# Block-sparse attention with a two-layer network behind it, on one core: the sampled numbers come in one piece, group 0's registers are loaded by two engines, weights are issued behind the first keys, and TensorE is given constant products in the opening

## The chip, the cores and the metric

The kernel runs on 1 core of one Trainium2 chip. The metric is the device time of one execution in microseconds (us), the median of several runs. The engines are named as in the profile: PE (TensorE, matmuls; PEld is its weight load), DVE (VectorE), ACT (ScalarE), POOL (GpSimd) and SP (SyncE, which here only loads registers and issues transfers). SPq, POOLq and PEq are the sequencers of these engines.

## The reference

Four batches, eight heads, 768 positions in 24 blocks of 32. A query block sees its neighbours, the first and the last block, and three sampled blocks; the first and the last query block see everything. The output goes through a two-layer network whose gate is h for h >= 1, 0 for h <= -1 and (h+1)^2/4 between.

```python
scores = scale * np.matmul(q, k.transpose(0, 1, 3, 2))
mask = np.abs(blk_i - blk_j) <= window
mask = mask | (blk_i == 0) | (blk_j == 0) | (blk_i == n_blocks - 1) | (blk_j == n_blocks - 1)
for qb in range(n_blocks):
    for kb in sampled_blocks[qb]:
        mask[qb * block:(qb + 1) * block, kb * block:(kb + 1) * block] = True
scores = np.where(mask, scores, -1000000000.0)
attn = np.exp(scores - np.max(scores, axis=-1, keepdims=True))
attn = attn / (np.sum(attn, axis=-1, keepdims=True) + 1e-09)
x = np.matmul(attn, v)           # then (4, 8, 768, 64) -> (3072, 512)
h = x @ w_in                     # (512, 2048), given in float64
g = np.where(pos, h, np.where(neg, 0.0, (h + beta) ** 2 / (4.0 * beta)))
out = g @ w_out                  # (2048, 512), given in float64
```

## The kernel before, in words

The work is cut into 24 **groups** of 128 queries (six for each batch), and the groups into nine **chunks** of two or three. Chunk 0 is the groups 0, 1 and 2. For a chunk the network runs 16 times over 128 of its 2048 hidden columns: `l1` (L628 to L630, 12 products into a bank `h` or `ob`), the gate (ACT L633, L635, L638; DVE L636; DVE or POOL L640) and `l2` (L647 to L649, into `oa`). The attention of the next chunk is interleaved with the network of this one. Chunk 0's attention has nothing to stand beside it but the conversion of the weights: it is the **opening**, and it ends with the first `l1` (67.61 us in the profile).

A group loads its queries `q` and, for the first group of a batch, the keys `kn` (two halves of 768 KB). The sampled block numbers are brought into `sreg` by a transfer (L182), and SP and POOL load 12 of them for a group into registers (L303). With these SP gathers value blocks into `va` or `vx` (L355, 64 KB each, 12 for a group), and POOL copies the sampled key blocks into `kr` (L345, 12 copies of 128x128 for a group, 6 into `kr0` and 6 into `kr1`). `ends` (L330) puts the first and the last key block into `kr`. Then two **score rounds** of matmuls go into two banks (`sa` and `sb`, or `oa1` and `oa2` for group 1), each followed by two minima (DVE L411), four exponentials (ACT L414), four transposes (PE L419) and copies of the turned tiles `pt` (L422). `values` multiplies with the values (L166, into `ob` or `oa0`), `xn` (DVE L570) divides, PE turns it back (L578), and `x` is written in a high (ACT L583) and a low part (DVE L584). `l1` of a chunk needs `x` of all its groups.

The weights come as float64. A **conversion** takes a tile of 1 MB (into one of three raw buffers: `stg0`, `stg1` and `out4`) through ACT L237, DVE L238, L240, L242 and L244, and splits it into a high part (ACT L247) and a low part (L249 on DVE or POOL). There are 16 of them, 8 for `w_in` and 8 for `w_out`; `w_out` also goes to DRAM as `wo_dram` for the later chunks.

The order of all steps on all engines is written out: `ORDER` is a packed list of step numbers that `Plan.order` unpacks, and the body runs the steps in it, so each engine's queue is that list in order. `BY` picks the engine of those steps that have a choice. The durations written at `pe(...)`, `act(...)` and so on are a planner's costs; nothing at run time reads them.

Of the kernel before, what the change touches and what calls it, by code (L numbers as in the profile page):

```python
# [24 lines left out]
NP = H // 2  # L25
# [48 lines left out]
def body(ctx, tc, q_t, k_t, v, samp, moe_w_in, moe_w_out, cst_in, out):  # L74
# [51 lines left out]
    sreg = sb.tile([1, NB * NR], I32, name="sreg")  # L126
# [46 lines left out]
    def constants():  # L173
# [84 lines left out]
    def group(b, t, key, wide, lead):  # L258
# [26 lines left out]
        if t == 0:  # L285
            for s in range(2):
                bs = slice(12 * s, 12 * s + 12)
                load(at(0) - lead + KNL[s], KN[:, bs], k_t[b, :, bs], ["first"] if g else (), [("kn", 3 * s + k) for k in range(3)], size=786432, by=None if g else ACT)
# [13 lines left out]
        def values_of(name, engine):  # L302
            vals[name] = nc.values_load_multi_w_load_instructions(  # L303
                sreg[0:1, blocks[0] * NR:(blocks[-1 if not mixed else 1] + 1) * NR], engines=[engine], min_val=0, max_val=NB - 1,
                skip_runtime_bounds_check_because="the sampled numbers are numbers of key blocks")[1]

        add("SP", 2.6, at(0) - lead + 3.4, lambda: values_of("SP", mybir.EngineType.SP), ["sreg"], [("val", "SP", g % 2)], 0.1)
        pool(1.6, at(0) - 1.6, lambda: values_of("POOL", mybir.EngineType.Pool), ["sreg"], [("val", "POOL", g % 2)], port=False, lat=1.1)
        for hf in range(nh):
# [32 lines left out]
            def keys(n=n, hf=hf):  # L342
                for m, val in enumerate(vals["POOL"][2 * NR * hf:2 * NR * hf + 2 * NR]):
# [3 lines left out]
            pool(1.72, at(0) - 1.5 + hf, keys, [("val", "POOL", g % 2)] + [("kn", s) for s in range(6)], [krn])  # L347
# [80 lines left out]
        if not mixed:  # L428
            for rnd in range(2):
                items = [(e, 2 * rnd + a, 256 * a, c, slice(32 * c, 32 * c + 32), i, c)  # L430
                         for a in range(2) for c, i in enumerate(blocks) for e in range(2)]
                pe((2.0, 1.5)[chunk] if narrow else 1.11, at(0.28 * rnd), lambda items=items: score_parts(items), score_reads, list(sn))
# [27 lines left out]
            pe(3.2 if chunk == 0 else 2.5 if chunk == 1 else 1.95, at(0.66), values, [("pt", p) for p in range(NP)] + va_r + vb_r, [on] + ([("vxdone", g - 1)] if spread else []))  # L460
# [134 lines left out]
    def moe(c, fis, t0, p, between):  # L595
# [5 lines left out]
        for k, fi in enumerate(fis):  # L601
            u = t0 + k * p
            for at_k, part in between:
                if at_k == fi:
                    attention(1, part)
# [106 lines left out]
    with tc.manual_schedule():  # L712
        for i in seq:
            plan.steps[i][3]()
# [6 lines left out]
BY = ("11200011100110000001011102100111000000000000001000000000000000000000001101100010011000110001101010101111010110"  # L721
      "11111111001110101010000000010111100000000000000000000000000000000000000000000000000000000000000000000000000000"
# [3 lines left out]
LEAD_0, LEAD_C, LEAD_W, LEAD_A, AHEAD = -33.59, 22.83, 5.97, 2.71, 7.29  # L726
L2 = 2.31
# [3 lines left out]
c-jrugMwf=5CFh*(#l)gwr$U>ZQHhO+qP}nwr$(qyZVb_V~sInoDq}PfSGOLnJ`9;H(^a7gC?5EXJVUhCYFh7qL?{msflhPn7O8e$!+4Bc_zGRXJVR!CNMEf  # L731
0+ZOBHc?GdGv6dKNlY@cz@#$EOe7P>EH;tNa#P+!G)qhhv(V%*-Ax6P+N3mTOmdUfEHdd#dz0Q|G!@NylfjfVl}sj+*%UFAO*WIo6gE{&U8rV?niVFisbWf-
l_t~_H>=DBli$=dZA^Ak+mthF%|=tq)H3T#8ME4KG9f01S!0sfI;NzlYjT=WX0vHv8k#01m-%V7nChmVX=`ej`li3BXPTO=rn%W}wwZ#akr`n6n8s#@8E86~
# [102 lines left out]
```

## Time and profile before

| | before |
|---|---|
| runs shown | 792.92, 794.43, 796.32 us; median 794.43 us |
| the profiled execution | 791.04 us, of which the span from the first to the last instruction is 789.3 us |
| PE busy | 753.5 us, 95% of the span |
| DVE, ACT, POOL busy | 363.5, 408.6, 138.6 us |
| mean granted clock of PE | 0.983 of full speed |

Idle time of PE and stretches at half clock are what a span can lose; the stages with most of both are read from windows of the trace. The page's shares of the whole span say little of the opening, which is less than a tenth of it.

### The profile page before, as it was taken

Reading aid. Unit: us, or ns where it says so; the run is one execution under the profiler, and the core shown is the slowest. Engines: PE = TensorE matmul, PEld = TensorE weight load, DVE = VectorE, ACT = ScalarE, POOL = GpSimd, SP = SyncE. Lnnn points to the kernel's source line nnn. Section 1 sums busy time; section 2 is a strip of 40 time slices with the busy share of each in tenths; the row PEclk is TensorE's granted clock in tenths of the full one; section 3 lists DMA queues with packets and bytes.
Section 4 is the critical chain, followed back from the end, with each engine's and each line's share of the span. In section 5 each row is a group of like instructions: output and inputs, shape, how many; then the busy total and the mean of one; then the engine's idle time right before and its main releaser. Section 6 shows DMA issues by size and latency. Waiting matters only on the chain.

```text
span 789.3 us, 21997 instructions
## 1 busy us (share of the span) xinstructions
PE 753.5 (95%) x8880; PEld 643.3 (82%) x8880; DVE 363.5 (46%) x695; ACT 408.6 (52%) x994; POOL 138.6 (18%) x379
## 2 busy tenths in 40 slices
PE   4788989999999999999999999999999999999997
PEld 3567868888878888888888888888888888888995
DVE  3956989633543334343443444344434242444332
ACT  1776677556755444444554454544545444546442
POOL 3242100304434100032220210032202020100000
PEclk7889999999999999999999999999999999999999
DMA  8998979587687365665466465755554636553554
GB/s 270 240 272 255 314 258 318 183 247 266 203 226 234 134 188 172 188 213 189 161 187 195 131 198 161 198 193 183 188 164 163 185 121 188 166 166 125 173 187 147
DMA packets 60457, 156.89 MB, mean 199 GB/s; under 512 B 8900, under 2 KB 9156, under 8 KB 60356
## 3 DMA queue, kind: packets, MB, share of 16 engines
q1 hardware_dynamic: 59924, 153.66, 61.9%
q10 hardware_dynamic: 432, 1.84, 0.7%
q8 instruction: 70, 1.15, 0.6%
q14 instruction: 31, 0.25, 0.1%
HBM read 140.78 MB, written 14.68 MB: 197 GB/s over the span
## 4 chain that ended last, share of the span: by engine, by line
PE 84%; DVE 5%; DMA 4%; ACT 3%; issue 3%; POOLq 1%; POOL 0%; SPq 0%; ACTq 0%
PE oa L647 11%; PE oa L649 10%; PE oa L648 10%; PE h L628 9%; PE h L630 9%; PE h L629 9%; PE sa L166 7%; PE ob L166 6%; PE ptb L419 5%; PE sb L166 1%; PE oa L628 1%; PE oa L630 1%; PE oa L629 1%; PE ptb L578 1%; DMA stg<-in_moe_w_out_dram 1%
## 5 line engine op out<-in xcount | busy, mean ns | idle before, releaser
L647 PE MATMUL oa<-w,gh 128*128 128x512 f32 x384 | 160.2, 417 | 1.7 <-DMA w<-wo_dram 1.3
L649 PE MATMUL oa<-w,gl 128*128 128x512 f32 x384 | 151.7, 395 | 0.1
L648 PE MATMUL oa<-w,gh 128*128 128x512 f32 x384 | 151.0, 393 | 0.0
L628 PE MATMUL h<-x,wi 128*128 128x384 f32 (+1 forms) x432 | 145.9, 338 | 2.2 <-DVE r L636 1.3
L633 ACT ACTIVATE r<-h,half_c 128x384 f32<-128x384 f32 (+1 forms) x108 | 60.8, 563 | 167.1 <-PE h L630 166.3
L630 PE MATMUL h<-x,wi 128*128 128x384 f32 (+1 forms) x432 | 141.4, 327 | 0.1
L629 PE MATMUL h<-x,wi 128*128 128x384 f32 (+1 forms) x432 | 140.7, 326 | 0.0
L636 DVE SCALAR_TENSOR_TENSOR r<-r,h 128x384 f32<-128x384 f32 (+1 forms) x108 | 56.8, 526 | 110.1 <-ACT r L635 109.2
L638 ACT CAST gh<-r 128x384 fp32r<-128x384 f32 (+1 forms) x144 | 68.5, 476 | 68.2 <-DVE r L636 60.9
L628 PEld LDWEIGHTS h<-x,wi 128*128 128x128 f32 x432 | 81.3, 188 | 10.2 <-issue 2.2
L647 PEld LDWEIGHTS oa<-w,gh 128*128 128x128 f32 x384 | 72.6, 189 | 20.8 <-issue 6.0
L337 POOL COPY kr<-kn 128x384 f32<-128x384 f32 x56 | 28.9, 547 | 341.1 <-PE sb L166 232.9
L649 PEld LDWEIGHTS oa<-w,gl 128*128 128x128 f32 x384 | 72.4, 189 | 17.1 <-DVE gl L640 0.6
L640 DVE TENSOR_TENSOR gl<-r,gh 128x384 fp32r<-128x384 f32 (+1 forms) x123 | 65.6, 534 | 42.4 <-ACT gh L638 38.6
L629 PEld LDWEIGHTS h<-x,wi 128*128 128x128 f32 x432 | 81.4, 188 | 2.0 <-DVE x L584 0.2
L648 PEld LDWEIGHTS oa<-w,gh 128*128 128x128 f32 x384 | 72.8, 190 | 10.8
L630 PEld LDWEIGHTS h<-x,wi 128*128 128x128 f32 x432 | 81.2, 188 | 0.4 <-issue 0.4
L345 POOL COPY kr<-kn 128x128 f32 x264 | 70.1, 315 | 43.2 <-PE sb L166 31.9
L635 ACT ACTIVATE r<-r 128x384 f32<-128x384 f32 (+1 forms) x144 | 70.8, 492 | 3.0
L166 PE MATMUL sa<-kr,q 64*32 64x256 f32 (+1 forms) x672 | 52.8, 382 | 9.7 <-POOL kr L345 8.3
L166 PE MATMUL sb<-kr,q 64*32 64x256 f32 (+1 forms) x672 | 52.3, 382 | 2.9 <-issue 2.6
L419 PE MATMUL ptb<-cst,p 128*128 128x128 f32 x328 | 51.2, 277 | 3.9 <-ACT pt L422 2.3
(143 smaller groups left out, 1244.2 us busy)
## 6 DMA issues: line engine op xcount, KB each, us to landing
w<-wo_dram SPq DMA_DIRECT2D x128, 512.0 KB, 3.4
va<-in_v_dram SPq DMA_DIRECT2D x240, 64.0 KB, 4.0
vb<-in_v_dram SPq DMA_DIRECT2D x38, 384.0 KB, 4.7
wo_dram<-w SPq DMA_DIRECT2D x16, 512.0 KB, 7.8
stg<-in_moe_w_in_dram SPq DMA_DIRECT2D x6, 1024.0 KB, 7.3
stg<-in_v_dram SPq DMA_DIRECT2D x8, 768.0 KB, 6.3
q<-in_q_t_dram SPq DMA_DIRECT2D x23, 256.0 KB, 4.4
stg<-in_moe_w_out_dram SPq DMA_DIRECT2D x5, 1024.0 KB, 8.5
```

Source lines behind the costliest of these rows:

```text
L166: PE.matmul(out=o, lhsT=l, rhs=r, start=start, stop=True, skip_group_check=True)
L345: POOL.tensor_copy(out=KR[n][:, m // NR, s:s + 1], in_=KN[:, bass.ds(val, 1)])
L419: PE.transpose(out=bank[:, k * 128:k * 128 + 128], in_=s, identity=ident)
L628: PE.matmul(out=h, lhsT=win(j, 0, fs), rhs=x[:, j, 0, 0:nt], start=(j == 0), stop=False)
L629: PE.matmul(out=h, lhsT=win(j, 0, fs), rhs=x[:, j, 1, 0:nt], start=False, stop=False)
L630: PE.matmul(out=h, lhsT=win(j, 1, fs), rhs=x[:, j, 0, 0:nt], start=False, stop=(j == NP - 1))
L635: act(GATE[size[c]][1], u, lambda r=r: ACT.activation(out=r, in_=r, func=AF.Square), [("r", n2)], [("r", n2)])
L638: act(GATE[size[c]][3], u, lambda r=r, gh=gh: ACT.copy(out=gh, in_=r), [("r", n2)], [("gh", n3)])
L640: return lambda: eng.tensor_tensor(out=gl, in0=r, in1=f(gh), op=ALU.subtract)
L647: PE.matmul(out=oa[t], lhsT=gh[:, ts], rhs=w[:, 0], start=(fi == fis[0]), stop=False)
L648: PE.matmul(out=oa[t], lhsT=gh[:, ts], rhs=w[:, 1], start=False, stop=False)
L649: PE.matmul(out=oa[t], lhsT=gl[:, ts], rhs=w[:, 0], start=False, stop=(fi == fis[-1]))
```

## The change

- `sreg` becomes twice as long and takes the sampled numbers as they lie in DRAM, 576 bytes in one piece, where before 72 words of 4 bytes were picked out of it. The registers are then loaded from every second word.
- Group 0's numbers for `kr1` are loaded into registers of ACT, and ACT makes the six copies into `kr1`. POOL loads six numbers for group 0 in place of twelve.
- `first`, on which the loads of weights and values wait in the planner's list, is now written by SP's register load for group 0 and not by the first transfer. So the weights are issued behind it; the keys and the queries of group 0 don't wait for it.
- `FILL` inserts 27 products of a constant tile (128x128 by 128x384, float32) ahead of six steps of PE: 7 before the first score round, then 5, 8, 2, 3 and 2. Nothing reads what they write.
- The costs of score rounds and of `values` in the opening are lower, and `ORDER` and `BY` are new tables: all queues have another order.

```diff
-    sreg = sb.tile([1, NB * NR], I32, name="sreg")
+    sreg = sb.tile([1, 2 * NB * NR], I32, name="sreg")
...
         def numbers():
-            SP.dma_start(out=sreg, in_=low(s_lin)[:, :, 0])
+            SP.dma_start(out=sreg, in_=s_lin.bitcast(I32))
             SP.dma_start(out=sraw, in_=s_lin.bitcast(I32).to_broadcast([128, 2 * NB * NR]))
 
-        add("SP", 2.2, -70, numbers, (), ["sreg", "sraw", "first"], size=80000)
-        load(-64, cst, cst_in, ["first"], ["cst"], size=200000)
+        add("SP", 1.2, -70, numbers, (), ["sreg", "sraw", "issued"], size=80000)
+        load(-64, cst, cst_in, ["issued"], ["cst"], size=200000)
...
+        nv = 2 * NR * nh
+        add("SP", 2.6, at(0) - lead + 3.4, lambda: values_of("SP", mybir.EngineType.SP, 0, nv), ["sreg"], [("val", "SP", g % 2)] + (["first"] if g == 0 else []), 0.1)
+        if g:
+            pool(2.4, at(0) - 1.6, lambda: values_of("POOL", mybir.EngineType.Pool, 0, nv), ["sreg"], [("val", "POOL", g % 2)], port=False, lat=0.4)
+        else:
+            pool(1.6, at(0) - 1.6, lambda: values_of("POOL", mybir.EngineType.Pool, 0, 2 * NR), ["sreg"], [("val", "POOL", 0)], port=False, lat=0.1)
+            act(1.6, at(0) - 1.6, lambda: values_of("ACT", mybir.EngineType.Activation, 2 * NR, nv), ["sreg"], [("val", "ACT", 0)])
...
+            by_act = g == 0 and hf == 1
+
+            def keys(n=n, hf=hf, who="ACT" if by_act else "POOL", copy=ACT.copy if by_act else POOL.tensor_copy):
+                for m in range(2 * NR):
                     s = m % NR + (5 if g == 1 else 0)
-                    POOL.tensor_copy(out=KR[n][:, m // NR, s:s + 1], in_=KN[:, bass.ds(val, 1)])
+                    copy(out=KR[n][:, m // NR, s:s + 1], in_=KN[:, bass.ds(vals[who][2 * NR * hf + m], 1)])
...
         for i in seq:
+            for _ in range(FILL.get(i, (0, 0))[0]):
+                PE.matmul(out=oa[FILL[i][1]][:, 0:HALF], lhsT=f(GH[0])[:, 0:128], rhs=f(GH[0]), start=True, stop=True)
             plan.steps[i][3]()
...
+FILL = {31: (7, 1), 38: (5, 1), 51: (8, 1), 82: (2, 1), 100: (3, 0), 136: (2, 1)}
```

PE's queue, from its first instruction to the transposes of group 0's second score round; `L724` is the constant product, `oa_112` is `oa1`, and the line numbers of the changed kernel are 7 to 12 higher.

```order
 L199 MATMUL h<-gh_71 128x384 x16
+L724 MATMUL oa_112<-gh_71 128x384 x7
 L166 MATMUL sa<-kr_80,q_77 32x160
...
-L419 MATMUL h<-cst,p_86 128x128 x2
-L419 MATMUL h<-cst,p_87 128x128 x2
+L724 MATMUL oa_112<-gh_71 128x384 x5
+L428 MATMUL h<-cst,p_86 128x128 x2
+L428 MATMUL h<-cst,p_87 128x128 x2
...
+L724 MATMUL oa_112<-gh_71 128x384 x8
```

Seven products were put between the warm-up and the first scores, five between these and the first transposes, eight ahead of the second round's transposes.

ACT's queue in the changed kernel behind its first transfers, up to group 0's four exponentials (L423; the `p` are the four tiles of the first round).

```order
L304 TENSOR_LOAD sreg
L337 COPY kr_81<-kn 128x256 x2
...
L354 COPY kr_81<-kn 128x128
...
L337 COPY kr_80<-kn 128x256 x2
L237 ACTIVATE stg_96<-stg_96 128x2x512
L423 ACTIVATE p_86,sm_97<-sa,nm_100 128x256
L423 ACTIVATE p_88,sm_97<-sa,nm_100 128x256
L237 ACTIVATE stg_95<-stg_95 128x2x512
L423 ACTIVATE p_87,sm_97<-sb,nm_100 128x256
L423 ACTIVATE p_89,sm_97<-sb,nm_100 128x256
```

Before, the same place read as follows.

```order
L330 COPY kr_80<-kn 128x256 x2
L330 COPY kr_81<-kn 128x256 x2
L237 ACTIVATE stg_95<-stg_95 128x2x512
L414 ACTIVATE p_87,sm_97<-sb,nm_100 128x256
L414 ACTIVATE p_89,sm_97<-sb,nm_100 128x256
L414 ACTIVATE p_86,sm_97<-sa,nm_100 128x256
L414 ACTIVATE p_88,sm_97<-sa,nm_100 128x256
L237 ACTIVATE stg_96<-stg_96 128x2x512
```

The register load and the copies into `kr1` are new on ACT (the copy's row stands six times there, an address row ahead of each), and the second weight tile's L237 moved from behind the four exponentials to between them.

SP's queue where group 2's queries (`q_77`) are loaded, in the changed kernel and then before; `vx_84` are group 1's values.

```order
L163 DMA out_76<-in_moe_w_out_dram 128x2x1024
...
L364 DMA vx_84<-in_v_dram 32x512
...
L364 DMA va<-in_v_dram 32x512
L163 DMA q_77<-in_q_t_dram 128x512
L163 DMA stg_95<-in_moe_w_out_dram 128x2x1024
```

```order
L163 DMA out_76<-in_moe_w_out_dram 128x2x1024
...
L355 DMA vx_84<-in_v_dram 32x512
L163 DMA vx_84<-in_v_dram 96x4x512
L163 DMA vx_84<-in_v_dram 32x4x512
L163 DMA q_77<-in_q_t_dram 128x512
```

The load of `q_77` moved ahead of group 1's neighbour values (`96x4x512`, 768 KB), of its two loads of end blocks (256 KB each; the other stood further up) and of one gather.

PE's queue at the end of the opening, with group 2's transposes back (`xn_94`); before, and then changed.

```order
L166 MATMUL sb<-mask,ones 32x2x96
L578 MATMUL h<-cst,xn_94 128x128 x4
L419 MATMUL ptb<-cst,p_88 128x128 x2
L419 MATMUL ptb<-cst,p_89 128x128 x2
L628 MATMUL h<-x_67,wi 128x384
```

```order
L166 MATMUL ob<-vx_85,pt_93 32x64 x16
L587 MATMUL h<-cst,xn_94 128x128 x4
L166 MATMUL sa<-kr_80,q_78 32x160
L166 MATMUL sa<-kn,q_78 32x96
L166 MATMUL sb<-kr_80,q_78 32x160
```

Before, group 3's second score round stood between group 2's `values` and its transposes back; now the transposes come first and the score round stands between them and the first `l1`.

## Rows read from the trace of the kernel before

**Rows 1.** Page: heading, and the granted clock in 40 slices.

```profile
span 789.3 us, 21997 instructions
...
PEclk7889999999999999999999999999999999999999
```

**Rows 2.** Windows by stage: start:end, busy us of each engine, clock, DMA share, GB/s.

```profile
0.00:13.70 13.70, 4.63 (x17) 4.31 (x17) 3.63 (x16) 2.61 (x5) 2.46 (x14) 0.80 0.81 262
13.70:67.60 53.90, 39.63 (x1032) 30.93 (x1032) 35.40 (x54) 32.33 (x88) 21.18 (x55) 0.83 0.90 248
67.60:143.70 76.10, 71.36 (x768) 61.19 (x768) 71.28 (x105) 54.09 (x111) 4.68 (x9) 0.98 0.84 277
...
160.00:770.00 610.00, 608.21 (x6849) 522.46 (x6848) 239.54 (x494) 305.05 (x762) 104.18 (x297) 1.00 0.58 183
770.00:789.30 19.30, 13.41 (x74) 10.87 (x72) 4.46 (x10) 4.90 (x11) 0.00 (x0) 1.00 0.43 141
```

**Rows 3.** Chain that ended last, 0 to 30 us: start us, us, what.

```profile
0.75 4.67 DMA sreg<-in_samp_dram
5.44 2.92 POOLq L303
8.43 2.74 POOLq L303
...
14.83 1.91 POOL kr L345 x4
...
18.87 0.70 DVE nm L411
...
21.12 0.66 PE h L419 x4
```

**Rows 4.** Timeline of ACT in the opening.

```profile
9.93 1.28 ACT L330 ACT_TABLE_LOAD   x1 [9.93 <-DMA kn<-in_k_t_dram]
11.22 1.32 ACT L330 COPY kr<-kn 128x256 f32<-128x256 f32 x4
...
21.41 1.17 ACT L237 ACTIVATE stg<-stg 128x1024 f32<-128x1024 f32 x1
```

**Rows 5.** DMA issues, 0 to 30 us: KB each, median us from issue to landing.

```profile
q<-in_q_t_dram ACTq DMA_DIRECT2D x1, 256.0 KB, 4.5
```

**Rows 6.** Chain that ended last, 30 to 68 us.

```profile
30.34 1.51 issue
...
32.56 6.88 DMA q<-in_q_t_dram
...
40.23 0.44 PE sa L166
...
42.99 1.06 PE h L419 x4
...
60.12 2.65 issue
...
65.16 1.06 PE h L578 x4
...
67.61 0.44 PE h L628
```

**Rows 7.** Windows: the longest stretch at half clock, and four such together.

```profile
9.20:19.40 10.20, 4.54 (x74) 3.35 (x74) 4.54 (x13) 3.76 (x6) 6.72 (x24) 0.55 1.00 303
...
sum 23.80, PE 17.31 PEld 14.23 DVE 10.76 ACT 11.86 POOL 14.38; mean PE 4.33 PEld 3.56 DVE 2.69 ACT 2.97 POOL 3.60
```

**Rows 8.** Timeline of PE: the warm-up.

```profile
1.33 4.63 PE L199 MATMUL h<-gh 128*128 128x384 f32 x16 [1.33 <-DVE ones L193]
```

**Rows 9.** Groups of DVE by shape, 67.6 to 143.7 us: busy us, mean ns.

```profile
L249 DVE TENSOR_TENSOR wi<-stg,wi 128x512 fp32r<-128x512 f32 x12 | 7.9, 683 | 0.0
...
L640 DVE TENSOR_TENSOR gl<-r,gh 128x384 fp32r<-128x384 f32 x11 | 6.0, 551 | 0.0
```

**Rows 10.** Waits of DVE, 13 to 143 us: total us, times, longest.

```profile
DVE stg L238 <- ACT stg L237: 6.6, 4, 2.9
```

More of the change, by code (lines that the diff above doesn't have):

```diff
@@ L287, in group @@
                 bs = slice(12 * s, 12 * s + 12)
-                load(at(0) - lead + KNL[s], KN[:, bs], k_t[b, :, bs], ["first"] if g else (), [("kn", 3 * s + k) for k in range(3)], size=786432, by=None if g else ACT)
+                load(at(0) - lead + KNL[s], KN[:, bs], k_t[b, :, bs], (), [("kn", 3 * s + k) for k in range(3)], size=786432, by=None if g else ACT)
         nh = len(blocks) // 2
@@ L300, in group, with values_of @@
         vals = {}
-        def values_of(name, engine):
-            vals[name] = nc.values_load_multi_w_load_instructions(
-                sreg[0:1, blocks[0] * NR:(blocks[-1 if not mixed else 1] + 1) * NR], engines=[engine], min_val=0, max_val=NB - 1,
+        def values_of(name, engine, lo, hi):
+            numbers = sreg.rearrange("a (n w) -> a n w", w=2)[:, blocks[0] * NR + lo:blocks[0] * NR + hi, 0]
+            got = nc.values_load_multi_w_load_instructions(
+                numbers, engines=[engine], min_val=0, max_val=NB - 1,
                 skip_runtime_bounds_check_because="the sampled numbers are numbers of key blocks")[1]
-        add("SP", 2.6, at(0) - lead + 3.4, lambda: values_of("SP", mybir.EngineType.SP), ["sreg"], [("val", "SP", g % 2)], 0.1)
-        pool(1.6, at(0) - 1.6, lambda: values_of("POOL", mybir.EngineType.Pool), ["sreg"], [("val", "POOL", g % 2)], port=False, lat=1.1)
+            vals.setdefault(name, {}).update(zip(range(lo, hi), got))
+        nv = 2 * NR * nh
[5 more added lines that the diff above has]
+            act(1.6, at(0) - 1.6, lambda: values_of("ACT", mybir.EngineType.Activation, 2 * NR, nv), ["sreg"], [("val", "ACT", 0)])
         for hf in range(nh):
@@ L431, in group @@
                          for a in range(2) for c, i in enumerate(blocks) for e in range(2)]
-                pe((2.0, 1.5)[chunk] if narrow else 1.11, at(0.28 * rnd), lambda items=items: score_parts(items), score_reads, list(sn))
+                pe(1.5 if narrow else 1.11, at(0.28 * rnd), lambda items=items: score_parts(items), score_reads, list(sn))
                 for e in range(2):
@@ L458, in values @@
                             first = False
-            pe(3.2 if chunk == 0 else 2.5 if chunk == 1 else 1.95, at(0.66), values, [("pt", p) for p in range(NP)] + va_r + vb_r, [on] + ([("vxdone", g - 1)] if spread else []))
+            pe(2.3 if chunk < 2 else 1.95, at(0.66), values, [("pt", p) for p in range(NP)] + va_r + vb_r, [on] + ([("vxdone", g - 1)] if spread else []))
             def recip():
@@ L602, in moe @@
             u = t0 + k * p
-            for at_k, part in between:
+            for at_k, one in between:
                 if at_k == fi:
-                    attention(1, part)
+                    attention(1, one)
             if c == 0 and opens and fi % 4 == 0:
```

102 lines of the change are left out of this document (50 added, 52 removed).

## The prediction

> **What bounds the kernel now.** I read the windows by stage first [rows 2]. From 160 to 770 us PE is busy for 608.21 of 610.00 us at full clock: that stage is as long as its matmuls, and the change alters none of them. The last 19.3 us keep their order. From 67.6 to 143.7 us, the network of chunk 0, PE is busy for 71.36 and DVE for 71.28 of 76.10 us: two engines are nearly full, and DMA has a share of 0.84. Only the stage before it is loose. From 13.7 to 67.6 us PE is busy for 39.63 of 53.90 us, so 14.3 us are idle, and the granted clock is 0.83 of full, so part of the busy time runs at half. What the change is worth is thus how much earlier the first `l1` starts, which is at 67.61 us [rows 6], less what the next stage gives back.
>
> Then I followed the chain. It begins with the sampled numbers: 4.67 us for `sreg`, two register loads on POOL of 2.92 and 2.74 us, the key copies until 14.83 + 1.91 = 16.74 us, the minima at 18.87 us and the first transposes at 21.12 us [rows 3]. Later it waits 6.88 us for group 2's queries, stops twice with no releaser shown (1.51 and 2.65 us), and ends with group 2's way back from 65.16 to 67.61 us [rows 6].
>
> The page's clock line has 7 and 8 in its first slices and 9 everywhere after [rows 1]. In the four stretches at half clock that I cut out, PE is busy for 17.31 of 23.80 us [rows 7]; at full clock the same work would take half, so 8.7 us is the most that a warm clock can give.
>
> **The change part by part.**
>
> *First scores.* The numbers in one piece: the price of one short transfer is not in the rows. It lies between nothing saved (4.67 us, if the queue ahead of it sets it) and a landing before the 4.5 us of the queries [rows 5]; I take 4.0 us, landing at 4.75. Six register values at half of the 2.92 us row are 1.5 us, the next twelve 2.74, so POOL is ready at about 9.0 in place of 11.17 us. But the copies also need the second half of the keys, which let ACT go at 9.93 us [rows 4]. With 72 words of four bytes and the weights no longer beside them, I take 9.7 us (8.7 to 9.9). POOL then makes 12 copies before group 0 is complete, group 1's six first by the order. At the pitch before, 24 copies from 11.2 to 16.74 us or 0.23 each, they take 2.8 us. ACT has four end copies of 1.32 us [rows 4] and six key copies. A register-addressed copy on ACT is not in the trace; between 0.23 (POOL's pitch) and 0.33 us (a quarter of 1.32) I take 0.3, so 3.1 us. The inputs are complete at 12.8 us. A score round at half clock took from 40.23 to 42.99 us, 2.76 us [rows 6], so it ends at 15.6 in place of 18.87 us: **3.3 us** earlier. Seven constant products lie in the 7.7 us between the warm-up's end (1.33 + 4.63) and the first score at 13.7. One costs between 0.29 us (the warm-up's 4.63/16, another format [rows 8]) and 0.83 us (three columns' worth of 1.11/4, from the transposes' 1.06 us for four at half clock [rows 6]); I take 0.4, so 2.8 us, and even 5.8 us fits.
>
> *First transposes.* Now the second weight tile's L237, 1.17 us [rows 4], stands between the exponentials. That gives back 1.2 us: **2.1 us** are left. The five products ahead of the transposes take 2 us in a wait that was 21.12 - 18.87 = 2.25 us. Were they at 0.83 us each, they would hold PE for 4.2 us and cost the whole of this gain.
>
> *Group 2's queries.* By the order rows their load is ahead of 768 + 256 + 256 + 64 KB that stood before it. At the 248 GB/s of this stage [rows 2] 1.38 MB are 5.5 us, and PE waited for just these queries. But in the new order group 1's second score round comes after group 2's first one, so one round (2.76 us at half clock) is still to be done there. 5.5 - 2.8 = **2.7 us**; the 2.1 us of the start are in it, not beside it, since both shorten the same path. Ends: 0.7 (if transfers, not order, set the pace) and 5.5.
>
> *Group 2's way back.* Before, the score round of group 3 came first, then the transposes back, and the first `l1` waited 67.61 - 65.16 = 2.45 us for ACT's and DVE's parts of `x`. Now the score round lies between, and covers that: **2.4 us** (0 to 2.4). The 2.65 us stop falls in the same score round; I leave it where it is.
>
> *Clock and constant products.* Twenty products from the first scores on are 8 us at 0.4, laid into 14.3 us of idle time. If they keep the clock up, at most 8.7 us come back. But much of what ran at half clock was followed by a wait for ACT, DVE or a transfer, which the clock doesn't shorten. I take a quarter: **2.2 us** (0 to 8.7).
>
> *DVE behind it.* Counted in the two orders up to the last `l2` of chunk 0, DVE has 27 splits L249 in place of 26, 14 low parts L640 in place of 12, and seven copies of `pt` in place of six. At 0.68 and 0.55 us [rows 9] that is 0.68 + 1.10 + 0.68 = **2.5 us** more, in a stage where DVE is busy for 94%. POOL's and ACT's relief there is worth nothing, since neither is full.
>
> *Sum.* -2.7 - 2.4 - 2.2 + 2.5 = -4.8 us. The profiled execution took 791.04 us with a span of 789.3, so it would be 786.2; it lies 3.4 us below the median of the runs shown, 794.43, which becomes 789.6. I say **789.5 us**. With every term at its good end it would be 14 us less, with every one at its bad end 2 us more; they won't all fall together.
>
> [...]
>
> **The rivals.**
>
> *The gain ends in the weights (0 to 2.5 us less).* DVE and DMA set the next stage: DVE has only 4.8 us of idle time in 76.1, and the raw tiles come when buffers are free. For it: both are near full [rows 2]. Against it: a start that is earlier for all engines shifts the whole stage, and what DVE has to do behind the first `l1` grew by little. Time: about 793.
>
> *All of the clock comes back.* Then the term is 8.7 in place of 2.2 us, the sum -11.3, the time 783. For it: the idle gaps that the products fill are the ones ahead of half clock. Against it: the chain of this stage passes through ACT, DVE and transfers as often as through PE.
>
> *Slower: weight tiles block ACT's queue.* L237 waits for its tile, and ACT works in order. In the new order it stands between group 0's exponentials and again ahead of group 1's; near the end DVE's L238 stands ahead of group 2's low part of `x`. Before, DVE waited for L237 four times, 2.9 us at the longest [rows 10]. If the three places each cost 2.9 us, that is 8.7 us, of which the sum holds 1.2; less the 4.8 us of the forecast, the kernel is 2.7 us slower, with the extra waits of PE at half clock some 4, so about 798. It decides from the point at which group 0's second tile lands later than about 19 us: from there on the first transposes are no earlier than before. Against it: that tile is asked for right behind SP's register load, the first tile and two gathers, some 10 us ahead of that point.
>
> *The numbers' form does nothing*, since the keys land at 9.9 us anyway: that takes 0.2 us off the first term and is inside the range.
>
> **How the numbers follow.** The forecast has 0.52, with a range of its own from 786 to 792; about seven tenths of it lie more than 4 us below 794.4. The gain that ends in the weights has 0.25, all of the clock 0.10, slower 0.13. A measurement of this kernel tells about 0.5%, or 4 us, from no change. Faster: 0.37 + 0.10 = 0.47. Same: 0.15 + 0.25 = 0.40. Slower: 0.13. The range 784 to 796 leaves out most of the full clock's case and most of the slower one, about 2 in 10.
>
> **What would show it.** Right: the first minima at about 15.6 us, the first transposes near 19, group 2's queries landing near 34, the first `l1` at 61 to 63 us, and a DVE that is at least as full behind it. The clock of the 13.7 to 67.6 us stage above 0.83 with a PE that is no less idle would be the products' work. Wrong: exponentials on ACT waiting behind an L237 that waits for its tile; the first `l1` earlier by 5 us and the end of chunk 0 not; or products at half clock that are still running when their transposes could start.

## The result and the profile after

The changed kernel takes **798.97 us** (median of 20 runs, 794.34 to 802.22), the kernel before 794.11 us beside it (20 runs, 788.58 to 799.75). The ratio is **1.0068, 95% interval 1.0048 to 1.0087**: slower by 0.7%, above the range of the prediction.

From the page of the changed kernel: the span, busy times, the granted clock in 40 slices, and the queue that brings TensorE's instructions (packets, MB, share).

```profile
span 795.9 us, 22112 instructions
...
PE 765.4 (96%) x8934; PEld 650.8 (82%) x8934; DVE 372.5 (47%) x705; ACT 408.5 (51%) x995; POOL 132.6 (17%) x368
...
PEclk9998999999999999999999999999999999999999
...
q8 instruction: 70, 1.15, 0.6%
```

The windows that answer to [rows 2], with the same columns:

```profile
0.00:13.70 13.70, 9.65 (x30) 7.45 (x30) 2.54 (x12) 4.20 (x12) 2.44 (x13) 1.00 0.80 259
13.70:67.60 53.90, 41.62 (x952) 31.12 (x952) 35.55 (x57) 28.93 (x79) 14.57 (x38) 0.93 0.83 230
67.60:143.70 76.10, 69.47 (x851) 59.29 (x852) 67.48 (x99) 52.24 (x108) 9.01 (x20) 0.96 0.84 269
160.00:770.00 610.00, 609.19 (x6905) 521.97 (x6904) 246.25 (x506) 304.38 (x761) 103.35 (x297) 1.00 0.60 186
```

The clock did what it was to do: 0.93 in the stage from 13.7 to 67.6 us, 0.83 before. All the same that stage is longer. The first `l1` starts at 74.2 us in place of 67.61, and from there to the end both kernels take the same 721.7 us (795.9 - 74.2, 789.3 - 67.6). So the 6.6 us that the two spans differ by are lost ahead of the first `l1`. The chain of the changed kernel up to there (start us, us, what), which answers to [rows 3] and [rows 6]:

```profile
0.75 1.25 DMA sreg<-in_samp_dram
2.01 2.65 SPq L304
...
7.10 12.52 DMA stg<-in_moe_w_in_dram
19.65 1.12 ACT stg L237
...
23.84 5.16 PE oa L724 x16
...
33.47 1.31 PE ob L166 x50
34.79 2.40 issue
37.19 2.35 PE ob L166 x78
...
41.07 2.29 issue
...
63.14 1.47 PE ob L166 x92
64.61 3.36 issue
67.97 1.30 PE ob L166 x36
```

The numbers land in 1.25 us in place of 4.67, but the chain no longer runs through them. It runs through the second weight tile, which lets ACT's `L237` go at 19.65 us between group 0's exponentials; through eight constant products (`L724`), 5.16 us or **0.645 us each**; and through three stops named issue, 8.05 us together, where before there were two of 1.51 and 2.65 us. Each stop lies inside a step whose operands are there: group 0's values stop after 50 of their 128 matmuls, group 2's after 92. (The chain has a fourth, of 0.82 us at 32.66 us, ahead of the first of group 0's values. It ends at 33.47 us, as group 0's last two gathers land, at 33.38 and 33.57 us.)

The half clock that the changed kernel has ahead of its first `l1` begins at the end of each of these three stops, or within its last 0.7 us, after TensorE has stood still. In these windows the clock is the third number from the end:

```profile
36.60:40.00 3.40, 2.81 (x94) 2.64 (x101) 1.79 (x3) 0.70 (x4) 0.00 (x0) 0.50 1.05 222
43.40:46.80 3.40, 3.40 (x46) 2.72 (x54) 1.19 (x2) 1.11 (x3) 0.00 (x0) 0.51 0.23 78
67.30:74.20 6.90, 5.44 (x116) 4.50 (x117) 4.37 (x6) 1.12 (x2) 1.05 (x3) 0.51 0.83 286
```

ACT's opening, as [rows 4]:

```profile
11.42 0.71 ACT L337 COPY kr<-kn 128x256 f32<-128x256 f32 x2 [7.37 <-DMA kn<-in_k_t_dram]
12.04 1.29 ACT L354 COPY kr<-kn 128x128 f32 x6
...
19.65 1.12 ACT L237 ACTIVATE stg<-stg 128x1024 f32<-128x1024 f32 x1 [1.09 <-DMA stg<-in_moe_w_in_dram]
20.67 0.46 ACT L423 ACTIVATE p<-sb,nm 128x256 f32<-128x256 f32 x1
```

The keys let ACT go at 11.42 us, later than the 9.93 of before. And the group of the products by its shape:

```profile
L724 PE MATMUL oa<-gh 128*128 128x384 f32 x54 | 18.5, 488 | 0.0
```

27 products are 54 matmuls: a product of float32 runs as two matmuls here, each with a weight load of its own (54 too). They are 18.5 us of TensorE, yet its busy time rose by only 11.9 us over the 753.5 of the kernel before, so 6.6 us of other work came back. TensorE's idle time (span less busy) fell from 35.8 to 30.5 us.

### The profile page after: what moved, and what is told of

Read it like the earlier page. It is cut to its first block, busy times and chain, and to the rows that moved or that the text cites. A ratio compares the mean times of both kernels' runs of the same rounds, so it can differ in the third digit from the quotient of the medians.

```text
span 795.9 us, 22112 instructions
## 1 busy us (share of the span) xinstructions
PE 765.4 (96%) x8934; PEld 650.8 (82%) x8934; DVE 372.5 (47%) x705; ACT 408.5 (51%) x995; POOL 132.6 (17%) x368
## 3 DMA queue, kind: packets, MB, share of 16 engines
q8 instruction: 70, 1.15, 0.6%
## 4 chain that ended last, share of the span: by engine, by line
PE 84%; DVE 6%; DMA 4%; ACT 3%; issue 2%; SPq 1%; ACTq 0%; DVEq 0%
PE oa L656 11%; PE oa L658 10%; PE oa L657 10%; PE h L637 9%; PE h L639 8%; PE h L638 8%; PE ob L166 7%; PE sa L166 6%; PE ptb L428 5%; DMA stg<-in_moe_w_in_dram 2%; PE oa L637 1%; PE sb L166 1%; PE oa L639 1%; PE oa L638 1%; PE ptb L587 1%
## 5 line engine op out<-in xcount | busy, mean ns | idle before, releaser
L649 DVE TENSOR_TENSOR gl<-r,gh 128x384 fp32r<-128x384 f32 (+1 forms) x129 | 70.2, 545 | 45.8 <-ACT gh L647 40.0
L344 POOL COPY kr<-kn 128x384 f32<-128x384 f32 x62 | 32.0, 547 | 326.9 <-PE sb L166 205.4
L657 PEld LDWEIGHTS oa<-w,gh 128*128 128x128 f32 x384 | 72.5, 189 | 10.7
L166 PE MATMUL sa<-kr,q 64*32 64x256 f32 (+1 forms) x672 | 49.9, 374 | 4.7 <-POOL kr L354 3.0
L423 ACT ACTIVATE p<-sa,nm 128x256 f32<-128x256 f32 x84 | 39.5, 474 | 19.1 <-DVE nm L420 18.4
```

The costliest lines, as they stand in the source:

```text
L166: PE.matmul(out=o, lhsT=l, rhs=r, start=start, stop=True, skip_group_check=True)
L649: return lambda: eng.tensor_tensor(out=gl, in0=r, in1=f(gh), op=ALU.subtract)
L657: PE.matmul(out=oa[t], lhsT=gh[:, ts], rhs=w[:, 1], start=False, stop=False)
```

## The experiments

**Theory A**: the new order of the DMA issues brings rows late. **B**: the products hold the path. **C**: weight tiles stand between group 0's softmax. **D**: the numbers' form decides the start. After the first four runs came **F**: the stops are waits for TensorE's own code. All ratios are to the kernel before, timed beside each kernel, with 95% intervals.

**e1: no products.**

```diff
-FILL = {31: (7, 1), 38: (5, 1), 51: (8, 1), 82: (2, 1), 100: (3, 0), 136: (2, 1)}
+FILL = {}
```

> Leaves out only the 27 constant products; order, loads and registers stay as in the changed kernel. Theory A (the order of the DMA issues makes group 0's and group 2's values late, 2.40 and 3.36 us of TensorE waiting): the first FFN matmul stays later than 72 us, and the time within 2 us of the changed kernel's, since the half-clock stretches come back while a few short waits get shorter. Theory B (the products themselves, 0.645 us each and 18.5 us in all, hold the path): the first FFN matmul comes 3 us or more earlier (71 us or below) and the time falls by 3 us or more. Both expect the half-clock time ahead of the first FFN matmul to grow from about 14 us towards the 23.8 us of the kernel before.

Measured: 800.48 us, ratio 1.0094 (1.0071 to 1.0118). The first `l1` is at 68.54 us, 5.7 earlier, and yet the end is not: from there on the kernel takes 726.8 us in place of 721.7. B is right about the first `l1` and wrong about the time. What TensorE waited for without the products (line and tile, total us, times, longest):

```profile
PE h L428 <- ACT p L423: 6.6, 5, 2.6
PE sb L166 <- issue: 5.3, 3, 3.2
PE ptb L428 <- ACT p L423: 4.7, 2, 3.1
PE h L637 <- DVE r L645: 2.6, 3, 1.2
PE ob L637 <- DVE r L645: 2.4, 2, 2.1
```

It waits 11.3 us for exponentials (3.0 + 1.4 on the same tiles in the kernel before), and later 5.0 us for the gate on DVE (1.3 before). The second transposes of group 0, ahead of which the eight products stand, start at 28.68 us here and at 28.84 with the products: at that place these fill a wait for exponentials. Ahead of the first `l1` e1 has one stop named issue inside a step, of 1.68 us, where the changed kernel has 8.05 us. Most of the 5.1 us behind it is one more such stop, of 3.19 us up to 91.82 us, and the half clock behind that:

```profile
91.82 0.29 PE L166 MATMUL sb<-kr,q 64*32 64x160 f32 x1 [3.19 <-issue]
92.00:95.50 3.50, 3.50 (x38) 3.20 (x27) 1.98 (x3) 1.46 (x2) 0.77 (x3) 0.51 0.92 336
```

So the new order is no faster without the products: they fill its waits, give the clock back (a mean granted clock of 0.990 with them, 0.978 in e1), and come out at about nothing.

**e2: SyncE's queue repaired.**

```diff
+        for some, ahead in MOVE:
+            for n in some:
+                seq.remove(n)
+                seq.insert(seq.index(ahead), n)
...
+MOVE = (((17, 19), 67), ((124, 122, 118, 125, 65, 119, 117, 64, 123, 115, 116, 114, 127, 120, 126), 203), ((222,), 145))
```

> The changed kernel, with SyncE's queue reordered: the last two gathers of group 0's values stand ahead of group 1's, and all of group 2's value gathers stand ahead of the load of group 3's queries, whose scaling on ScalarE moves to group 2's second round. Theory A: the waits of 2.40 us ahead of group 0's values and of 3.36 us ahead of group 2's values go, the first FFN matmul comes at 68 to 71 us in place of 74.2, and the time falls by 3 to 5 us, to about that of the kernel before. Theory B (products) and theory C (a weight tile's absolute value between group 0's exponentials): those waits are only the last of several, another takes their place, and the time moves by less than 1.5 us.

Measured: 798.57 us, 1.0078 (1.0047 to 1.0109). The stops stay: 2.98, 3.22 and 2.27 us, after the same matmuls, although group 0's last gathers were issued at 25.8 us in place of 28.8. A falls for these stops.

**e3 and e4: one part in the order before.** e3 adds the 27 products ahead of the same steps (one bank that they write is still in use there, so part of the attention is wrong); e4 loads the numbers in one piece.

```diff
+FILL = {30: (7, 1), 37: (5, 1), 50: (8, 1), 81: (2, 1), 99: (3, 0), 135: (2, 1)}
...
-            SP.dma_start(out=sreg, in_=low(s_lin)[:, :, 0])
+            SP.dma_start(out=sreg, in_=s_lin.bitcast(I32))
```

> The kernel before, with the same 27 constant products ahead of the same matmul steps and nothing else changed. If the clock is what the waiting in the opening costs, half-clock time falls from 23.8 us by 10 us or more and the time by 2 to 4 us (791 or less beside 794). Theory B: 18.5 us of products where TensorE waited some 12 us in all lengthen the opening; the time rises by 2 us or more. If the products only use idle time, and the clock's gain is small because TensorE then waits for others, the time stays within 1.5 us.

> The kernel before, with the sampled numbers loaded in one piece and the registers read two words apart; one engine still reads group 0's registers. The numbers land about 3 us earlier (near 2.0 us in place of 5.4), so POOL has its twelve registers near 8 us, and its key copies wait for the keys (near 10 us) instead. Theory D (this edit is worth the difference at the first scores): first minima about 1 us earlier, time 0.5 to 1.5 us lower. Rival: the weight tiles and values that are released with the numbers go out earlier too and push the keys back, as in the changed kernel (11.4 us): first minima no earlier, time within 1 us or higher.

Measured: e3 799.39 us, 1.0067 (1.0042 to 1.0091): in the old order, whose waits are shorter, float32 products cost 5 us (with the reservation on that bank, whose readers they may wait for). e4 791.99 us, 1.0004 (0.9982 to 1.0025), first minima at 17.33 in place of 18.87 us, first `l1` at 68.05 in place of 67.61: the start is won and lost again behind it.

**What a stop is.** The page counts 70 packets and 1.15 MB in the queue of TensorE's instructions, for 2 x 8,934 matmuls and weight loads: 255 to a packet, 16 KB each. So I counted where in TensorE's stream each stop lies. Ahead of group 0's values the changed kernel has 593 instructions: 33 of the warm-up, 22 products of 4, 440 of scores and 32 of transposes. After 50 matmuls and their weight loads that is number 693; before, it was 505 + 2 x 95 = 695 (95 of the 128 matmuls ran ahead of the 1.51 us).

| kernel | number in the stream (us of the stop), up to 70 us |
|---|---|
| before | 695 (1.51), 1961 (2.65) |
| changed | 693 (2.40), 949 (2.29), 1965 (3.36) |
| e4 | 441 (2.26), 1455 (0.49), 1961 (2.11) |
| e1 | 1965 (1.68) |
| g1 | 693 (0.89), 949 (4.59), 1965 (2.08) |
| f1 | 951 (1.60), 1457 (1.23), 1961 (1.15) |
| f2 | 949 (3.41), 1205 (2.10), 1457 (2.51), 1965 (2.77) |
| g4 | 441 (0.90), 951 (1.83), 1455 (1.14), 1961 (0.87) |
| i1 | 443 (3.07), 1459 (0.94), 1963 (2.56) |
| i3 | 439 (0.55), 695 (4.50), 1961 (2.82) |

Other kernels, other steps, the same few numbers, some 253 apart in this count, beside the page's 255 to a packet: I read them as the ends of blocks of code, one to a packet. (Waits ahead of the first of group 0's values are left out: the changed kernel's 0.82 us, and 1.50 us in e1, 0.53 in g1 and 0.59 in f2. They stay with that step when its number changes, as waits for its rows do.) In the changed kernel a packet of that queue is on the DMA engines in the quarter microsecond from 34.50 us (from 40.75, from 65.25), and TensorE goes on at 37.19 (43.36, 67.97), 2.4 to 2.7 us later. The 20 traces have 83 stops named issue of more than 0.4 us. Five stand ahead of the first of group 0's values; the other 78 all stand at numbers of this series, and in each TensorE goes on 2.2 to 2.9 us after a packet of this queue has started.

These stops take 0.5 to 4.7 us. In the kernel before and in the changed one all seven of them stand inside scores or values (L166), stretches of short matmuls: between its first two stops the changed kernel passes 256 numbers of the stream, 693 to 949, in 3.9 us (37.19 to 41.07).

**f1 and f2: the same work, its code shifted.** Tiny products behind the warm-up, 64 in the kernel before, 48 in the changed one, where TensorE waits for keys.

```diff
                 PE.matmul(out=hb[:, 0:HALF], lhsT=warm[:, 0:128], rhs=warm, start=True, stop=True)
+            for _ in range(48):
+                PE.matmul(out=hb[0:32, 0:16], lhsT=warm[:, 0:32], rhs=warm[:, 0:16], start=True, stop=True)
```

> The kernel before, with 64 tiny products (128 TensorE instructions) more behind the warm-up, where TensorE waits 7.75 us for keys: they delay nothing and move every later TensorE instruction 128 places back in its stream. Theory F (the stops named issue come where the engine's code arrives in blocks of 256 instructions and the next block is not there): stops stay at the same numbers of the stream (about 440, 695, 950, 1203, 1456, 1709, 1962, the remainder by 256 falling slowly from 185 to 167), so the stops of 1.51 us (inside group 0's values) and 2.65 us (inside group 3's scores) go from the matmuls where they were, and others come 128 instructions earlier in the work; the time moves by up to 3 us either way. Rival (a stop is a wait for those matmuls' own data): the stops stay at the same matmuls, time within 1 us.

> The changed kernel, with 48 tiny products (96 instructions) more behind the warm-up, inside the wait of 3.0 us ahead of the first scores. Theory F: the stops of 2.40, 2.29 and 3.36 us leave the matmuls where they were and stand again at about 695, 950 and 1962 of the stream, which are now the start of group 0's values, the start of group 2's scores and the first half of group 2's values; what they cost together differs from 8.05 us. Rival (late value rows, theory A): stops at the same matmuls, time within 1 us of the changed kernel's.

Measured: f1 789.78 us, 0.9977 (0.9953 to 1.0001); f2 **803.06 us, 1.0130 (1.0098 to 1.0161)**, an interval wholly above that of the changed kernel. First scores are at 13.87 and 13.82 us (13.70 and 14.02 without the shift). From the timelines of TensorE, f1 and then f2, each row with the stop ahead of it:

```profile
33.48 0.27 PE L166 MATMUL oa<-kn,q 64*32 64x96 f32 x1 [1.60 <-issue]
...
59.44 0.88 PE L166 MATMUL ob<-vx,pt 128*32 128x64 f32 x48 [1.15 <-issue]
```

```profile
39.96 0.27 PE L166 MATMUL sa<-kn,q 64*32 64x96 f32 x1 [3.41 <-issue]
45.88 0.27 PE L166 MATMUL oa<-kn,q 64*32 64x96 f32 x1 [2.10 <-issue]
54.05 0.83 PE L166 MATMUL oa<-vx,pt 128*32 128x64 f32 x42 [2.51 <-issue]
```

In f1 group 0's values run through without a stop, and the stop in group 3's scores is gone; others stand at the same numbers, in group 1's scores and group 2's values. F holds, its rival falls. 96 instructions that do nothing made the changed kernel some 4 us slower.

**f3, g2, h3: group 0's softmax first.** f3 moves the weight tiles' steps behind it, with 2 products for 8 ahead of step 51; g2 has e2's moves as well; h3 has both and no products.

```diff
+MOVE = (((158,), 39), ((159,), 160), ((43,), 162), ((47, 45), 165))
```

> The changed kernel with the weight tiles' steps out of the way of group 0's softmax: the second tile's absolute value behind both pairs of first exponentials, the second minimum ahead of the tile's last merge, the two copies of weights behind the second round's exponentials, and 2 products in place of 8 ahead of group 0's last transposes. Theory C (these are what made the opening late): group 0's last transposes 2.5 to 3.5 us earlier (by 27 us in place of 29.9), the first FFN matmul 2 us or more earlier and the time 2 us lower. Theory F: the start of group 0's values moves up, but TensorE then reaches the next block of its code sooner and stops longer there (at about 695 of the stream), so that the time falls by less than 1.5 us.

> Both repairs of the changed kernel's order at once (group 0's softmax ahead of the weight tiles' steps, 2 products for 8, and the gathers of SyncE's queue put forward). With only the first, group 0's values waited for the two late gathers until 35.05 us; with only the second, they were there and TensorE stopped for code. Theory A with C (each repair was hidden by what the other leaves): group 0's values start by 32 us without waiting for rows, the first FFN matmul comes by 70 us, and the time falls by 3 us or more against the changed kernel. Theory F: the stop at about 695 of the stream takes most of it; the time falls by less than 2 us.

> The changed kernel with no products and with both repairs of its order (group 0's softmax ahead of the weight tiles' steps, the gathers put forward). If the new order costs its 6 us through the exponentials (TensorE waited 11.7 us for them without products, 4.7 in the kernel before) and the late rows (1.5 us), those waits fall by 4 us or more and the time comes to 795 us or less. If the loss lies in what the order does later (the waits for the gate on VectorE, 5.0 us beside 1.3) or in the stops for code, the time stays at 798 or above.

Measured: 797.23 us, 1.0076 (1.0043 to 1.0109); 799.19, 1.0066 (1.0038 to 1.0093); 803.88, 1.0137 (1.0105 to 1.0169). In f3 group 0's values could start at 31.5 us but wait 3.51 us, until the two late gathers, issued from 29.3 us on, have landed (5.7 and 5.5 us): here A is right. In g2 the rows are there, and the same step stops 3.36 us at number 693. In h3 the exponentials cost 8.3 us in place of 11.7, but queries, rows and the half clock cost more, and one stop at number 2727 takes 4.68 us. Each wait that was taken away stood ahead of another; no repair of a place brought the time back.

**g1: the products' time taken out, their instructions left** (two tiny products for each).

```diff
-            for _ in range(FILL.get(i, (0, 0))[0]):
-                PE.matmul(out=oa[FILL[i][1]][:, 0:HALF], lhsT=f(GH[0])[:, 0:128], rhs=f(GH[0]), start=True, stop=True)
+            for _ in range(2 * FILL.get(i, (0, 0))[0]):
+                PE.matmul(out=oa[FILL[i][1]][0:32, 0:16], lhsT=GH[0][:, 0:32], rhs=GH[0][:, 0:16], start=True, stop=True)
```

> The changed kernel with each constant product replaced by two tiny ones (32 columns of weights, 16 of data), which are as many TensorE instructions (4), so that every later instruction keeps its number in the stream, but take next to no time. Theory F: the stops for code stand at the same numbers (about 695, 950, 1962) as in the changed kernel, and the time differs by what the products' 18.5 us cost less what their clock gives back. Theory B (the products are what made it slower): the time falls by 3 us or more against the changed kernel. Rival to B: as in the kernel with no products at all, the half clock comes back and the time stays within 2 us.

Measured: 796.72 us, 1.0038 (1.0007 to 1.0069). That overlaps the changed kernel's interval: in this order the products cost something between nothing and some 5 us. Stops of 0.89 and 4.59 us stand at 693 and 949, the numbers of the changed kernel. g1 and e1 differ by these tiny instructions alone, 16 of whose matmuls take 0.73 us. Yet g1's first `l1` is at 72.81 us and e1's at 68.54, with 7.56 and 1.68 us of stops ahead of it: in this order the place of the blocks moves the first `l1` by 4 us. The end does not follow it, since e1 has its stop of 3.19 us later.

**g3 and h1: less data on the DMA engines.** One and two weight tiles are not loaded (the expectations say what is wrong in the output); h1 also clears the buffer that is left unwritten, on DVE, before 14 us.

```diff
+        if n in (2, 3):
+            add("SP", 0.47, key - LEAD_C, lambda: None, ["first"], rr)
+        else:
+            load(key - LEAD_C, rw, words, ["mask"] if j == 2 else ["first"], rr, size=1048576)
```

> The changed kernel without the load of one 1 MB weight tile (the third staging use, issued at 29.66 us; its conversion runs on the old words, so a part of the output weights is wrong). Same instructions on TensorE. Theory F with queueing (a block of code is itself a transfer that stands behind the data): the stops at about 695 and 950 of the stream (2.40 and 2.29 us) shrink by half or more together. Rival (a block takes its fixed time whatever the load): they stay within 0.5 us each.

> The changed kernel without the loads of two 1 MB weight tiles (issued at 26.66 and 29.66 us; the words that they would bring are zeros or old, so a part of the output weights is wrong). Queueing (a block of code stands behind the data in the DMA engines): where TensorE reaches the ends of its blocks (about 695 and 950 of the stream) the DMA engines are less busy, the packet with the next block follows sooner after the end of the block before, and the two stops, 2.40 and 2.29 us in the changed kernel, come to 2.5 us or less together. If a block takes its time whatever the load, they stay at 4 us or more together.

Measured: g3 798.73 us, 1.0057 (1.0032 to 1.0083), stops of 1.87 and 4.04 us; h1 one run of 798.65 us, stops of 0.77 and 4.31. g3's sum of 5.9 us fits neither of its two expectations; h1's of 5.1 us is above the 4 us that stands for a time that does not depend on the load. The first stop of h1 shrank where the DMA share from 30 to 34 us was 0.44 (1.05 in the changed kernel); the second is longer. From the start of the packet to TensorE's going on it is 2.75 and 2.91 us in h1, 2.66 and 2.48 in the changed kernel: less load did not shorten that. What decides when a packet goes out is not shown.

**f4 and g4: cheap products at the two certain waits, in the order before.** g4 has the numbers in one piece too, and 44 for 40.

```diff
+            for _ in range(FILL.get(i, 0)):
+                PE.matmul(out=oa[1][:, 0:HALF], lhsT=GH[0][:, 0:128], rhs=GH[0], start=True, stop=True)
             plan.steps[i][3]()
...
+FILL = {30: 40, 37: 10}
```

> The kernel before, with 40 products in float32r (about 0.16 us each at full clock, from the warm-up's) ahead of the first scores and 10 ahead of the first transposes, the two places where TensorE stands idle (7.75 and 2.29 us) whatever comes. If full clock in the scores and values of groups 0 and 1 is worth what they are busy for longer at half clock, TensorE's busy time less the products falls by 3 us or more and the time by 1.5 us or more, below the kernel before. Theory F: what the clock gives back comes again as stops for code, because a block is used up sooner: busy time falls but stops grow, and the time stays within 1.5 us.

> The kernel before with the numbers in one piece and 54 products in float32r (44 ahead of the first scores, 10 ahead of the first transposes): the two parts that cost nothing alone, together. If their gains add, first scores near 12.9 us and full clock in groups 0 and 1: time 787 to 790, 3 us or more below the kernel before. Theory F: first scores come earlier but the block bounds, 108 instructions later in the stream, take part of it; time within 2 us of the kernel with products alone (789.6).

Measured: f4 789.62 us, 0.9985 (0.9961 to 1.0009); g4 **788.63 us, 0.9937 (0.9911 to 0.9962)**, the fastest. First transposes of g4 at 18.85 us, first `l1` at 65.69. What its TensorE waits for:

```profile
PE ob L166 <- issue: 2.6, 2, 1.7
PE sa L166 <- ACT q L366: 2.1, 1, 2.1
PE sa L166 <- issue: 2.0, 2, 1.1
PE ptb L419 <- ACT pt L422: 1.9, 1, 1.9
PE h L419 <- DVE x L584: 1.8, 1, 1.8
PE oa L166 <- issue: 1.8, 1, 1.8
```

The 7.7 us for keys are gone from the list, since products fill them.

**h2: g4 with 32 tiny products more** (f2's loop, `range(32)`).

> The fastest kernel so far (numbers in one piece, 54 float32r products, 788.6 us) with 32 tiny products (64 instructions) more behind the warm-up, in time in which TensorE waits for keys. Theory F: the stops for code, 6.1 us of its waits, leave the matmuls where they were and fall 64 instructions earlier in the work; the time moves by 1 to 3 us, either way. Rival (where the blocks end does not matter for the time): within 1 us.

Measured: 794.85 us, 1.0025 (1.0004 to 1.0046), 6 us more than g4. Not all of it is the blocks' place: g4's products already reach the first scores, so these were not hidden, and the first transposes are 0.9 us later (19.75). The stops named issue grow from 6.7 to 10.7 us, 3.5 of them behind 200 us, in the later chunks.

**i1, i2, i3: the remaining parts in the order before.** i1: numbers, and ACT for the second half of group 0's registers and keys; i2: that with g4's products; i3: numbers, and SyncE's registers ahead of the constants and the weights.

```diff
+                who, copy = ("ACT", ACT.copy) if g == 0 and hf == 1 else ("POOL", POOL.tensor_copy)
...
+MOVE = (((22,), 157),)
...
+MOVE = (((8,), 1),)
```

> The kernel before with the numbers in one piece, and the registers and key copies of group 0's second half on ScalarE in place of POOL (its six copies stand ahead of the first weight tile's absolute value). Nothing else of the order changes. If the first term of the prediction is right in itself (POOL's copies hold the first scores), group 0's second half of keys is ready about 2 us earlier than with the numbers alone, first minima come 1.5 us or more earlier, and the time falls by 1 to 2 us. If the weight tile that the copies push back, or a stop for code, gives it back: within 1 us of the kernel before.

> The same two parts with the 54 float32r products (numbers, registers by two engines, full clock; the order of the kernel before). If the parts add up: 1 to 2 us below the 788.6 us of numbers and products. Theory F: the stops for code stand at the same numbers of the stream as there (about 440, 950, 1456, 1962) and grow by what the start gains, time within 1.5 us of 788.6.

> The kernel before with the numbers in one piece and SyncE's registers of group 0 loaded ahead of the constants and the first weight tile, as in the changed kernel: the weight tile goes out near 5 us in place of about 2 us, with the gathers behind it. If this is what pushed the first keys back (11.4 us in the changed kernel, 10.5 with the numbers alone), keys land after 11 us and the time rises by 1 us or more; if it puts the weights behind the keys, keys land before 10 us and first scores come 0.5 us or more earlier than the 12.84 us of the numbers alone.

Measured: i1 792.12 us, 0.9979 (0.9949 to 1.0009), first minima at 16.77 us; i2 789.22, 0.9948 (0.9922 to 0.9973); i3 792.17, 0.9988 (0.9960 to 1.0015), first minima at 16.80. Each has its first minima 2 us earlier than the kernel before; in i1 and i3 longer stops follow (3.07 us at number 443, 4.50 at 695). In i3 the keys let ACT go at 9.97 us, though the first weight tile goes out at 5.13 us, as in the changed kernel, and gathers from 7.2 us on. None of these parts is slow by itself.

## Why the prediction was wrong

**What was slower.** All nine kernels timed in the new order, with products or without, mended or with a load left out, have ratios of 1.0038 to 1.0137; in the old order the numbers alone and with one more part (e4, i1, i3) lie between 0.9979 and 1.0004, and the float32 products alone (e3) at 1.0067. So the loads and registers do not cost it. The new order is enough for the loss, without products too, and in the old order the float32 products are enough; together they cost no more than either. Summed over the tiles, TensorE's waits in the profiled executions were, in us:

| | keys | exponentials | gate on DVE | issue | idle, all | busy |
|---|---|---|---|---|---|---|
| before | 8.3 | 4.7 | 1.3 | 4.6 | 35.8 | 753.5 |
| changed | 3.0 | 4.7 | 4.7 | 9.3 | 30.5 | 765.4 |
| e1 | 7.0 | 11.7 | 5.0 | 7.0 | 41.0 | 754.3 |

Which place of the order costs it is not shown: f3, g2, e2 and h3 each mended places and left the time. Nor do the stops explain all of it: those of the series come to 4.9 us in e1 and, with one of 0.51 us at 243.93 us, to 4.7 in the kernel before, and e1 is 6 us longer.

**Point by point.** *First scores* (3.3 us): the mechanism was right, the landing of the keys was not. I took 9.7 us; they let ACT go at 11.42. Why is open. In i3 the first weight tile goes out as late as here and the keys land by 9.97 us; but the changed kernel's ACT also asks for the queries ahead of both halves of the keys (before: between them), and its second weight tile goes out at 7.10 us, in i3 at 10.42. First minima at 16.81, 2.1 us earlier, not 3.3. i1 and i3 got as much in the old order.

*First transposes* (2.1 us): here the slower rival's mechanism came true. The second tile landed at 19.6 us, past the 19 us named as the point that decides; `L237` waited 1.09 us, and the last two of the four transposes start at 21.27 us, where all four started at 21.12 before: nothing gained. Its price of 2.9 us at each of three places was not what made 798: taking it away (f3) left the time where it was.

*Group 2's queries* (2.7 us): they landed at 34.1 us, as forecast, but its first scores started at 39.54 in place of 40.23, behind group 0's values, which stood still from 34.79 to 37.19. 0.7 us, not 2.7.

*Group 2's way back* (2.4 us): covered as said, no wait is left between transposes and first `l1`. But "the 2.65 us stop falls in the same score round; I leave it where it is" is **the step that failed**. The two stops without a releaser were in the rows, and I carried them over as if they belonged to their matmuls. They belong to numbers in TensorE's stream, and the products' 108 instructions (and another order) put other work there: 3.36 us in group 2's values, 8.05 in all, 3.9 more than before, and stretches at a clock of 0.50 to 0.51 follow each. The 3.9 us are more than half of the 6.6 us; f2 (the time) and g1 beside e1 (the first `l1`) show that the place of the blocks alone moves either by some 4 us. The rest of the 6.6 us stays open.

*Products*: 0.645 us in place of 0.4, since a float32 product is two matmuls; the upper bound of 0.83 held it (the 1.11 us that it is worked out from stands in none of the rows; with the row's 1.06 us it is 0.80). They take 18.5 us in place of 10.8. The eight ahead of step 51 end at 29.00 us, but without them (e1) the transposes behind them come only 0.16 us earlier.

*Clock* (2.2 us, 0 to 8.7): 6.6 us of other busy time came back, so the rival in which all of the clock comes back had the better reading. The products' 18.5 us used it up: the changed kernel has 10.5 us less idle time than e1 and 11.1 us more of busy time.

*DVE* (2.5 us): 372.5 us busy over the whole run, 9.0 more than before, and 3.4 us more of TensorE's waits for the gate. The waits came as forecast, their cost did not show: behind the first `l1` both kernels take 721.7 us.

*The sum*: -4.8 us forecast, +6.6 in the profiled pair, +4.9 in the medians. That the slower rival's 798 us lies next to the measured time is luck, since what it priced was not what cost it.

## What to carry to other kernels

A wait that a trace puts down to nothing can have an owner, as the 78 stops had here: count where it lies in the engine's instruction stream before calling it fixed, and count added instructions as a possible cost, since here they moved the matmuls at which TensorE stops, and some 4 us with them (f2 beside the changed kernel). Filler that keeps the clock (0.990 in f4, 0.983 before) belongs where the engine waits whatever comes, in the cheaper format of the two tried: a float32r product took 0.18 us in g4, a float32 one 0.645 (54 of the first and a shorter load gave 0.6%). When a change comes with a new order, run its parts in the old order first.

## What was not expected of the hardware

- TensorE stops for 0.5 to 4.7 us at numbers of its stream that are some 253 apart and the same within 4 in every kernel here (439 to 443, 693 and 695, 1961 to 1965), and not at each of them. Its instructions come in packets of 16 KB, 255 to a packet by the page (70 packets, 1.15 MB), and it goes on 2.2 to 2.9 us after such a packet has started (78 stops in 20 traces).
- A float32 product of 128 x 128 by 128 x 384 took 0.645 us at a granted clock of 1.00 (23.84 to 29.00 us of the changed kernel), as two matmuls; in float32r 44 of them took 8.07 us in g4, 0.18 each.
- The transfer of 144 words in one piece took 1.25 us in the changed kernel, that of 72 words two apart 4.67 in the kernel before.
